# Two units per attention step on TensorE: outputs and scores of a pair taken together every eight places

## The chip, the cores and the metric

The kernel runs on one core of one Trainium2 chip. The metric is the device time of one launch in microseconds (us): 609.71 us before the change, the median of three runs (609.52 to 609.72). One further run was profiled; it took 609.88 us, and its profile spans 608.1 us from the first to the last instruction.

## The reference

Chunked attention with memory keys, then a dense two-layer block with a leaky rectifier (negative values are scaled by alpha). Everything is in float32.

```python
B, H, S, D = 4, 8, 768, 64          # chunk 32, 16 keys to the left, 8 to the right, 8 memory keys
for c in range(S // 32):
    q_c    = q[:, :, 32*c : 32*c+32]
    k_full = concat(mem_k, k[:, :, 32*c-16 : 32*c+40])     # cut at the ends of the sequence
    scores = q_c @ k_full.T / 8
    a      = exp(scores - max(scores)); a = a / (sum(a) + 1e-9)
    out[:, :, 32*c : 32*c+32] = a @ v_full
x = out.transpose(0, 2, 1, 3).reshape(3072, 512)
h = x @ w_in                                               # 512 -> 2048
g = max(h, 0) + alpha * min(h, 0)
y = g @ w_out                                              # 2048 -> 512
```

## The kernel before

The 3072 tokens are cut into 8 **blocks** of 384. A block's attention is cut into 4 **units** of two heads each, so there are 32 units; unit u belongs to block u // 4. The dense block works on one block of tokens and one 128-wide slice f of the 2048 hidden channels at a time; such a (block, f) is a **place**, and `ORDER` lists the 128 places. Blocks 0 and 1 are interleaved at first; from place 32 on each block has 16 places in a row. `PLACE` gives a place's number.

At a place TensorE makes an **up** (12 matmuls of 128x384, line 638, into one of two PSUM banks, h0 or h1 by the place's parity), ScalarE and VectorE make g from it (lines 647 and 650, then 656 and 660 split it into a high and a low part), and TensorE makes a **down** (9 matmuls of 128x512, line 668, into three banks o0 to o2). Full float32 precision comes from three products of high and low parts. From place `FIRST_RUN` on, places are asked for in runs of four: four ups follow each other, then the downs; four pairs of buffers for g's parts (`NSUM`) allow it.

Units 0 to 7 are done at the start by other functions (`windows`). Units 8 to 31 are each done in this way, in the midst of the places:

- **scores**: `head_products` (line 292) is 24 small float32 products (the trace shows each as two, 48 matmuls), one head into bank s0, the other into s1.
- **softmax**: `scores` (lines 301 to 331): VectorE hides the keys that lie outside (302 or 304), takes the maximum (313) for each head, negates it (316); ScalarE takes six exponentials (323), with their sums.
- **weights** and **turn** (lines 333 to 371): sums are inverted, GpSimd multiplies (343), and VectorE transposes the result in 14 pieces (364).
- **outputs**: `value_products` (line 378) is 8 products (16 matmuls in the trace) into bank `a`; `split` (lines 411 and 415) copies them into a high and a low part, the x that the ups of the unit's block read.

`attend` (line 385) is one **step** of TensorE: the outputs of an old unit, where there is one that is due, and then the scores of a new one. `BEGIN` and `LATER` say at which place a unit begins; its outputs are due `DUE_VALUES` = 4 places later. So from place 33 on there is a step every four places.

The order is fixed when the kernel is built. `Plan` (line 103) takes the steps with an engine, an estimated cost, keys read and written, and a `rest` (how much work is left from the place at which the step is due). `send` plays this through: on each engine it takes, of the steps that could run earliest, the one with the most work behind it. What comes out is a fixed order for each engine; each engine works in that order and waits on semaphores. A step that is due at a smaller place number goes ahead of others.

Of the kernel before, what the change touches and what calls it, by code (L numbers as in the profile page):

```python
# [9 lines left out]
F32 = mybir.dt.float32  # L10
F32R = mybir.dt.float32r
AF = mybir.ActivationFunctionType
ALU = mybir.AluOpType
AX = mybir.AxisListType
# [4 lines left out]
P = 128  # L19
B, H, S, D = 4, 8, 768, 64  # L20
NM = 8
CH, LEFT, RIGHT = 32, 16, 8
WIN = LEFT + CH + RIGHT
KW = WIN + NM
TQ = 96
NJ = TQ // CH
# [3 lines left out]
NT = BT // TQ  # L30
NPAIR = H // 2
# [4 lines left out]
NEG = -3.0e38  # L36
SCALE = 1.0 / 8.0
# [22 lines left out]
PE, DVE, ACT, POOL, SP = "PE", "DVE", "ACT", "POOL", "SP"  # L60
# [6 lines left out]
NJOINT, LAG = 9, 1  # L67
# [6 lines left out]
PLACE = {x: i for i, x in enumerate(ORDER)}  # L74
# [1 line left out]
PAIR = 4.7  # L76


BEGIN = {2: (4, 6, 8, 10)}

NSUM = 4
RUN, FIRST_RUN = 4, 32
LATER = (-3, 1, 5, 9)


STIR = (8, 2, 1)

DUE_WEIGHTS, DUE_VALUES = 3, 4


NWIN, NSET = 2 * NPAIR, 4
# [68 lines left out]
def body(ctx: ExitStack, tc: tile.TileContext, qvw, kw, first, w_in, w_out, alpha, out):  # L160
    nc = tc.nc
# [47 lines left out]
    def rest(place):  # L209
        return (len(ORDER) - place) * PAIR  # L210

    def begins(u):

        blk, i = divmod(u, NPAIR)
        if blk < 2:
            return blk
        return PLACE[(1, NJOINT - 1) if blk == 2 else (blk - 1, 0)] + BEGIN.get(blk, LATER)[i]

    def due(u, later=0):

        return rest(begins(u) + later)

    def sets(u):

# [2 lines left out]
    def e_keys(u):  # L227
        return [("e", u % 2, n) for n in range(NJ * 2)]

    def den_keys(u):  # L230
        return [("den", u % 3, n) for n in range(NJ * 2)]
# [15 lines left out]
    def load_v(u):  # L247
        blk, pr = divmod(u, NPAIR)

        def load():  # L250
            state[u]["v"] = ld.tile([P, NT, 2, D], F32, name="v_t")
            nc.sync.dma_start(out=state[u]["v"],
                              in_=qvw[blk, pr, :, BT:].rearrange("p (t h d) -> p t h d", t=NT, h=2))

        step(SP, 0.75, load, writes=["v"])

    def stir(t, num):

# [3 lines left out]
    def score_products(u):  # L262
# [8 lines left out]
        for n in range(2 * NJ):  # L271
            for i in range(2):
# [5 lines left out]
                    start=True, stop=True,  # L278
                )

    def head_products(u):

        st = state[u]
        st["s"] = [ps_s.tile([P, 512], F32, name="s_ps", tag=f"s{h2}")[:, :NJ * KW].rearrange("p (n k) -> p n k", n=NJ)
                   for h2 in range(2)]
        for n in range(NJ):
            for g in range(4):
                t, j = SLOT[(g, n)]
                c = t * NJ + j
                for h2 in range(2):  # L290
                    rows = slice(h2 * D, (h2 + 1) * D)
                    nc.tensor.matmul(  # L292
                        out=st["s"][h2][g * CH:(g + 1) * CH, n],
                        lhsT=qs[sets(u)][rows, c * CH:(c + 1) * CH],
                        rhs=kbs[sets(u)][rows, t, STARTS[j]:STARTS[j] + KW],
                        start=True, stop=True,
                    )

    def hide(u, s):

        if u // NPAIR % 2 == 0:
            nc.vector.memset(s[0:CH, 0, ..., 0:LEFT], NEG)
        else:
            nc.vector.memset(s[3 * CH:4 * CH, NJ - 1, ..., KW - RIGHT:KW], NEG)

    def scores(u):
        st = state[u]

        def top(h2):
            if h2 == 0:  # L310
                st["mx"] = sm.tile([P, NJ, 2], F32, name="mx", tag=f"mx{u % 3}")
            hide(u, st["s"][h2])
            nc.vector.tensor_reduce(out=st["mx"][:, :, h2], in_=st["s"][h2], axis=AX.X, op=ALU.max)

        def negate():
            nc.vector.tensor_scalar(out=st["mx"], in0=st["mx"], scalar1=-SCALE, scalar2=None, op0=ALU.mult)  # L316

        def exps(i):
            if i == 0:
                st["e"] = at.tile([P, NJ * 2, KW], F32, name="e", tag=f"e{u % 2}")  # L320
                st["den"] = sm.tile([P, NJ * 2, 1], F32, name="den", tag=f"den{u % 3}")
            n, h2 = divmod(i, 2)
            nc.scalar.activation(out=st["e"][:, i], in_=st["s"][h2][:, n], func=AF.Exp, scale=SCALE,  # L323
                                 bias=st["mx"][:, n, h2:h2 + 1], accum_out=st["den"][:, i])

        for h2 in range(2):
            step(DVE, 0.46, partial(top, h2), writes=[("s", h2), ("mx", u % 3)], rest=due(u))
        step(DVE, 0.16, negate, writes=[("mx", u % 3)], rest=due(u))
        for i in range(NJ * 2):
            step(ACT, 0.54, partial(exps, i), reads=[("s", i % 2), ("mx", u % 3)],  # L330
                 writes=[("e", u % 2, i), ("den", u % 3, i)] if i else e_keys(u) + den_keys(u), rest=due(u))

    def weights(u):
        st = state[u]

        def guard():
            nc.vector.tensor_scalar(out=st["den"], in0=st["den"], scalar1=1e-9, scalar2=None, op0=ALU.add)

        def inverse():
            nc.vector.reciprocal(out=st["den"], in_=st["den"])  # L340

        def scale():
            nc.gpsimd.tensor_tensor(out=st["e"], in0=st["e"], in1=st["den"].broadcast_to([P, NJ * 2, KW]),  # L343
                                    op=ALU.mult)

        def spread():
            nc.scalar.copy(out=zeroed["e2"][:, :, NM:NM + CH], in_=st["e"][:, :, :CH])

        step(DVE, 0.16, guard, writes=den_keys(u), rest=due(u, DUE_WEIGHTS))
        step(DVE, 0.19, inverse, writes=den_keys(u), rest=due(u, DUE_WEIGHTS))  # L350
        step(POOL, 0.86, scale, reads=den_keys(u), writes=e_keys(u), rest=due(u, DUE_WEIGHTS))
        step(ACT, 0.37, spread, reads=e_keys(u), writes=["e2"], rest=due(u, DUE_WEIGHTS))

    TURNS = [(g, j, n0, n1, t0) + piece
             for g in range(4)
# [4 lines left out]
    def turn(u):  # L360
        st = state[u]

        def go(g, j, n0, n1, t0, src, half, quad):
            nc.vector.transpose(  # L364
                out=pts[u % NPT][quad * CH:(quad + 1) * CH, j, t0:t0 + n1 - n0].rearrange("p t h q -> p (t h) q"),
                in_=(st["e"], zeroed["e2"])[src][g * CH:(g + 1) * CH, 2 * n0:2 * n1, half * CH:(half + 1) * CH],
            )

        for i, x in enumerate(TURNS):
            step(DVE, 0.37 if x[3] - x[2] > 1 else 0.235, partial(go, *x), reads=["e2"] if x[5] else e_keys(u),  # L370
                 writes=[("pt", u % NPT, i)], rest=due(u, DUE_WEIGHTS))

    def value_products(u):
        st = state[u]
        st["a"] = ps_a.tile([P, 512], F32, name="a_ps", tag="a")
        for t in range(NT):
            for h2 in range(2):
                nc.tensor.matmul(  # L378
                    out=st["a"][h2 * D:(h2 + 1) * D, t * TQ:(t + 1) * TQ],
                    lhsT=st["v"][:, t, h2, :],  # L380
                    rhs=pts[u % NPT][:, :, t, h2, :],
                    start=True, stop=True,
                )

    def attend(place, olds, news):

        def products():
            for u in olds:
                value_products(u)
            for u in news:  # L390
                head_products(u)

        reads, writes = [], []
        for u in olds:
            reads += ["v"] + [("pt", u % NPT, i) for i in range(len(TURNS))]
            writes.append("a")
        for u in news:
            reads += [("q", sets(u)), ("k", sets(u))]
            writes += [("s", 0), ("s", 1)]
        step(PE, 0.85 * len(olds) + 0.67 * len(news) - (0.2 if olds and news else 0.0), products, reads=reads, writes=writes,  # L400
             rest=rest(place))

    def split(u, ak="a"):

# [325 lines left out]
    def unit_begins(u):  # L730
        if u < NWIN:
            windows(u)
        else:
            scores(u)
        if u < NWIN and u + NSET < NWIN:
            load_first(u + NSET)
        elif u >= NWIN - NKB and u + NKB < NU:
            load_unit(u + NKB)
# [11 lines left out]
    step(POOL, 3.0, zero, writes=["e2"] + [("pt", i, j) for i in range(NPT) for j in range(len(TURNS))] + [("ew", i) for i in range(NPT)])  # L750
    for f in range(NF - NSET, NF):
        load_w(f)
    load_v(NWIN)

    todo = {}
    for u in range(NWIN, NU):
        todo.setdefault(begins(u), []).append((u, 0))
        todo.setdefault(begins(u) + DUE_WEIGHTS, []).append((u, 1))
        todo.setdefault(begins(u) + DUE_VALUES, []).append((u, 2))
    down = done = None  # L760
    o_ps = {}
    for blk, f in ORDER:
# [13 lines left out]
        if olds or news:  # L776
            attend(PLACE[blk, f], olds, news)
        for u in olds:
            split(u)
            if u + 1 < NU:  # L780
                load_v(u + 1)
        for u in news:
            unit_begins(u)
        for u, part in now:
            if part == 1:
                weights(u)
                turn(u)
        o = o_ps.setdefault((blk, f1), [])
        down = partial(add_down, o)
        if f == f1 - 1:  # L790
# [57 lines left out]
```

## Time and profile before

| | |
|---|---|
| median of three runs | 609.71 us |
| the profiled execution | 609.88 us, span 608.1 us |
| TensorE matmul (PE) | 600.4 us busy, 99% of the span |
| VectorE (DVE) | 399.0 us, 66% |
| ScalarE (ACT) | 212.2 us, 35% |
| GpSimd (POOL) | 33.9 us, 6% |
| granted TensorE clock | 1.0 |

In the profile a row of a group names the line, the engine, the operation, output<-input and the count, then after the bar the busy time, the mean duration and the idle time before the group's instructions. PEld is TensorE's weight load. A matmul's duration in the trace is longer than the time until the next may start, since matmuls overlap; so what a piece of work costs TensorE is read from the start of one piece to the start of the next, as the chain of work that ended last lists it.

### The profile page before, as it was taken

The numbers are of one execution on the slowest core, as the hardware profiler recorded it, in microseconds if no ns is written. First come the engines' busy times: TensorE is split into PE (matmuls) and PEld (weight loads), VectorE is DVE, ScalarE is ACT, GpSimd is POOL, SyncE is SP. The second block draws the span as 40 slices with busy tenths as digits, with TensorE's granted clock in tenths as the row PEclk, the third lists the DMA queues.
The fourth block names the chain that finished last, engine by engine and source line by source line (L and its number), as shares of the span: only waits on it lengthen the run. The fifth ranks groups of instructions, "written<-read, shape, count | busy, mean of one in ns | idle before, by whom it ended". The sixth has DMA issues, their size and how long they took to land.

```text
span 608.1 us, 11545 instructions
## 1 busy us (share of the span) xinstructions
PE 600.4 (99%) x4618; PEld 532.0 (87%) x4622; DVE 399.0 (66%) x1012; ACT 212.2 (35%) x596; POOL 33.9 (6%) x61
## 2 busy tenths in 40 slices
PE   8999999999999999999999999999999999999997
PEld 5789989888888898998889998898998898999986
DVE  5888999868887667476665756577555767434331
ACT  3688887545222222421223221222222222121111
POOL 3410000001000000000000000000000000000000
PEclk9999999999999999999999999999999999999999
DMA  8999400014131011311012111111112000010001
GB/s 335 355 408 408 176 0 1 23 43 150 51 119 49 3 48 50 101 50 50 3 49 101 50 50 50 53 50 50 50 50 87 18 16 19 1 52 1 0 1 52
DMA packets 20934, 48.99 MB, mean 81 GB/s; under 512 B 2448, under 2 KB 5520, under 8 KB 20880
## 3 DMA queue, kind: packets, MB, share of 16 engines
q1 hardware_dynamic: 20880, 48.25, 22.4%
q8 instruction: 36, 0.59, 0.4%
q14 instruction: 18, 0.15, 0.1%
HBM read 41.95 MB, written 6.29 MB: 79 GB/s over the span
## 4 chain that ended last, share of the span: by engine, by line
PE 94%; DMA 3%; DVE 2%; ACT 0%; issue 0%; SPq 0%; ACTq 0%
PE h_ps L638 44%; PE o_ps L668 43%; PE a_ps L378 3%; PE s_ps L292 3%; DMA w_t<-w_in 2%; DMA early<-first 1%; DVE w_t L571 0%; DVE xl L415 0%; SPq L427 0%; DVE den L458 0%; DVE a L575 0%; DVE w_t L567 0%; DVE mx L446 0%; DVE e L450 0%; PE s_ps L274 0%
## 5 line engine op out<-in xcount | busy, mean ns | idle before, releaser
L638 PE MATMUL h_ps<-xh,w 128*128 128x384 f32 x1024 | 260.9, 335 | 0.3 <-DVE w L586 0.3
L668 PE MATMUL o_ps<-w,gh 128*128 128x512 f32 x768 | 238.2, 391 | 0.0
L638 PEld LDWEIGHTS h_ps<-xh,w 128*128 128x128 f32 x1024 | 185.4, 188 | 2.6 <-DVE w L586 0.6
L638 PE MATMUL h_ps<-xl,w 128*128 128x384 f32 x512 | 174.6, 341 | 0.1
L668 PEld LDWEIGHTS o_ps<-w,gh 128*128 128x128 f32 x768 | 144.1, 188 | 29.1
L647 ACT ACTIVATE g<-h_ps 128x384 f32<-128x384 f32 x128 | 64.1, 501 | 289.8 <-PE h_ps L638 289.6
L650 DVE SCALAR_TENSOR_TENSOR g<-g,rise,h_ps 128x384 f32<-128x384 f32 x128 | 78.4, 613 | 130.0 <-ACT g L647 129.0
L668 PE MATMUL o_ps<-w,gl 128*128 128x512 f32 x384 | 149.8, 390 | 0.0
L364 DVE STREAM_TRANSPOSE pt<-e 32x192 f32<-32x192 f32 (+1 forms) x336 | 99.5, 301 | 6.7 <-POOL e L343 1.8
L638 PEld LDWEIGHTS h_ps<-xl,w 128*128 128x128 f32 x512 | 96.1, 188 | 4.5 <-DVE xl L415 0.3
L668 PEld LDWEIGHTS o_ps<-w,gl 128*128 128x128 f32 x384 | 72.1, 188 | 14.1
L660 DVE TENSOR_TENSOR gl<-g,gh 128x384 fp32r<-128x384 f32 x128 | 70.1, 548 | 3.8 <-ACT gh L656 1.5
L323 ACT ACTIVATE e<-s_ps,mx 128x64 f32<-128x64 f32 x144 | 43.0, 324 | 6.6 <-DVE mx L316 6.6
L343 POOL TENSOR_TENSOR e<-e,den 128x384 f32<-128x384 f32 x24 | 19.9, 830 | 455.6 <-DVE den L340 435.3
L656 DVE CAST gh<-g 128x384 fp32r<-128x384 f32 x104 | 37.3, 360 | 7.7 <-PE o_ps L668 3.3
L323 ACT ACTIVATION_READ_ACCUMULATOR e<-s_ps,mx 128x1 f32 x144 | 31.3, 218 | 0.0
L715 ACT COPY o_t<-o_ps 128x512 f32<-128x512 f32 x21 | 12.2, 588 | 48.5 <-PE o_ps L668 47.3
L378 PEld LDWEIGHTS a_ps<-pt,v_t 128*64 128x64 f32 x384 | 16.6, 136 | 6.1 <-issue 6.1
L411 ACT CAST xh<-a_ps 128x384 fp32r<-128x384 f32 x32 | 15.4, 481 | 16.8 <-PE a_ps L378 14.8
L378 PE MATMUL a_ps<-pt,v_t 128*64 128x96 f32 x384 | 21.1, 252 | 0.0
L559 ACT ACTIVATE a<-w_t 128x1024 f32<-128x1024 f32 (+1 forms) x18 | 18.8, 1050 | 4.1 <-DMA w_t<-w_in 3.0
L575 DVE SCALAR_TENSOR_TENSOR a<-a,w_t 128x1024 int32<-128x1024 int32 (+1 forms) x18 | 19.8, 1102 | 0.2
(52 smaller groups left out, 283.6 us busy)
## 6 DMA issues: line engine op xcount, KB each, us to landing
w_t<-w_in SPq DMA_DIRECT2D x16, 512.0 KB, 10.2
w_t<-w_out SPq DMA_DIRECT2D x16, 512.0 KB, 10.2
qk<-kw SPq DMA_DIRECT2D x24, 272.0 KB, 3.8
v_t<-qvw SPq DMA_DIRECT2D x24, 256.0 KB, 2.7
out<-o_t SPq DMA_DIRECT2D x24, 256.0 KB, 2.1
early<-first SPq DMA_DIRECT2D x8, 656.0 KB, 6.2
qk<-qvw SPq DMA_DIRECT2D x24, 192.0 KB, 3.9
early<-first SPq DMA_DIRECT2D x8, 256.0 KB, 6.9
```

Source lines behind the costliest of these rows:

```text
L323: nc.scalar.activation(out=st["e"][:, i], in_=st["s"][h2][:, n], func=AF.Exp, scale=SCALE, bias=st["mx"][:, n, h2:h2 + 1], accum_out=st["d ...
L343: nc.gpsimd.tensor_tensor(out=st["e"], in0=st["e"], in1=st["den"].broadcast_to([P, NJ * 2, KW]), op=ALU.mult)
L364: nc.vector.transpose(out=pts[u % NPT][quad * CH:(quad + 1) * CH, j, t0:t0 + n1 - n0].rearrange("p t h q -> p (t h) q"), in_=(st["e"], zer ...
L378: nc.tensor.matmul(out=st["a"][h2 * D:(h2 + 1) * D, t * TQ:(t + 1) * TQ], lhsT=st["v"][:, t, h2, :], rhs=pts[u % NPT][:, :, t, h2, :], sta ...
L559: nc.scalar.activation(out=d["a"].bitcast(F32), in_=t[:, :, :, 1].bitcast(F32), func=AF.Copy, scale=REBIAS)
L575: nc.vector.scalar_tensor_tensor(out=d["a"], in0=d["a"], scalar=3, in1=d["t"][:, :, :, 1], op0=ALU.logical_shift_left, op1=ALU.bitwise_or)
L638: nc.tensor.matmul(out=h["ps"][:, :BT], lhsT=ws[f, 0][:, wk, k * P:(k + 1) * P], rhs=xs[first + k][xk], start=(k == 0 and n == 0), stop=(k ...
L647: nc.scalar.activation(out=h["g"], in_=h["ps"][:, :BT], func=AF.Relu, scale=-1.0)
L650: nc.vector.scalar_tensor_tensor(out=h["g"], in0=h["g"], scalar=rise[:, f:f + 1], in1=h["ps"][:, :BT], op0=ALU.mult, op1=ALU.add)
L656: copy(out=h["gh"], in_=h["g"])
L660: nc.vector.tensor_tensor(out=h["gl"], in0=h["g"], in1=h["gh"].bitcast(F32), op=ALU.subtract)
L668: nc.tensor.matmul(out=o_ps[tt], lhsT=h[gk][:, tt * P:(tt + 1) * P], rhs=ws[f, 1][:, wk], start=(f == first_f and i == 0), stop=(f == last ...
```

## The change

From unit 12 on (block 3), two units are taken together. `attend` is called with up to two old and two new units: outputs, outputs, scores, scores. The scores of both units lie side by side in the banks s0 and s1 (`banks`), so that one memset and one maximum per head serve both, and one negation. The second unit's outputs go to bank h1, one of the two banks of the ups; they leave it by the same `split`. Pairs begin at the places 0 and 6 of block 2 and, later, 4 places before and 4 after a block's start, so there is a step every eight places. It is asked for 0.2 places ahead of its place, where it was asked for at its place. V has two buffers in place of one. `FIRST_RUN` goes from 32 to 24, and the estimated costs of the steps and the due times are set anew.

```diff
-BEGIN = {2: (4, 6, 8, 10)}
+BEGIN = {2: (4, 6, 8, 10), 3: (0, 6)}
...
-RUN, FIRST_RUN = 4, 32
-LATER = (-3, 1, 5, 9)
+RUN, FIRST_RUN = 4, 24
+FIRST_FRONT = 12
+LATER = (-4, 4)
...
-DUE_WEIGHTS, DUE_VALUES = 3, 4
+DUE_WEIGHTS, DUE_VALUES = {1: 3, 2: 4}, {1: 4, 2: 8}
...
+    def size(u):
+        return 1 if u < 3 * NPAIR else 2
...
-        return rest(begins(u) + later)
+        return rest(begins(u) + later + (1.8 if u >= FIRST_FRONT else 0))
...
-            state[u]["v"] = ld.tile([P, NT, 2, D], F32, name="v_t")
+            state[u]["v"] = ld.tile([P, NT, 2, D], F32, name="v_t", tag=f"v{u % 2}")
...
+    def banks(us):
+        n = len(us)
+        ss = [ps_s.tile([P, 512], F32, name="s_ps", tag=f"s{h2}")[:, :n * NJ * KW].rearrange("p (u n k) -> p u n k", u=n, n=NJ)
+              for h2 in range(2)]
+        for i, u in enumerate(us):
+            state[u]["s"] = [s[:, i] for s in ss]
+        state[us[0]]["all"] = ss
...
-    def scores(u):
+    def scores(us):
...
-            hide(u, st["s"][h2])
-            nc.vector.tensor_reduce(out=st["mx"][:, :, h2], in_=st["s"][h2], axis=AX.X, op=ALU.max)
+            s = state[us[0]]["all"][h2]
+            hide(us[0], s)
+            nc.vector.tensor_reduce(out=d["mx"][:, :, :, h2], in_=s, axis=AX.X, op=ALU.max)
...
-            step(DVE, 0.46, partial(top, h2), writes=[("s", h2), ("mx", u % 3)], rest=due(u))
-        step(DVE, 0.16, negate, writes=[("mx", u % 3)], rest=due(u))
-        for i in range(NJ * 2):
-            step(ACT, 0.54, partial(exps, i), reads=[("s", i % 2), ("mx", u % 3)],
-                 writes=[("e", u % 2, i), ("den", u % 3, i)] if i else e_keys(u) + den_keys(u), rest=due(u))
+            step(DVE, 0.26 + 0.21 * len(us), partial(top, h2), writes=[("s", h2), mk], rest=due(us[0]))
+        step(DVE, 0.17, negate, writes=[mk], rest=due(us[0]))
+        for u in us:
+            for i in range(NJ * 2):
+                step(ACT, 0.54, partial(exps, u, i), reads=[("s", i % 2), mk],
+                     writes=[("e", u % 2, i), ("den", u % 3, i)] if i else e_keys(u) + den_keys(u), rest=due(u))
...
     def value_products(u):
         st = state[u]
-        st["a"] = ps_a.tile([P, 512], F32, name="a_ps", tag="a")
+        pool, tag = (ps_h, "h1") if u % size(u) else (ps_a, "a")
+        st["a"] = pool.tile([P, 512], F32, name="a_ps", tag=tag)
...
             for u in olds:
                 value_products(u)
+            if news:
+                banks(news)
             for u in news:
                 head_products(u)
...
-        step(PE, 0.85 * len(olds) + 0.67 * len(news) - (0.2 if olds and news else 0.0), products, reads=reads, writes=writes,
-             rest=rest(place))
+        step(PE, 0.31 + 0.53 * len(olds) + 0.48 * len(news), products, reads=reads, writes=writes,
+             rest=rest(place - (0.2 if (olds + news)[-1] >= FIRST_FRONT else 0)))
...
-        todo.setdefault(begins(u) + DUE_WEIGHTS, []).append((u, 1))
-        todo.setdefault(begins(u) + DUE_VALUES, []).append((u, 2))
+        todo.setdefault(begins(u) + 1, []).append((u, 1))
+        todo.setdefault((begins(u) + DUE_VALUES[size(u)] if size(u) == 1 or u + 2 >= NU else begins(u + 2)), []).append((u, 2))
...
         for u in olds:
-            split(u)
-            if u + 1 < NU:
-                load_v(u + 1)
-        for u in news:
-            unit_begins(u)
+            split(u, "h1" if u % size(u) else "a")
+            if u + 2 < NU:
+                load_v(u + 2)
         for u, part in now:
             if part == 1:
                 weights(u)
                 turn(u)
+        for u in news:
+            unit_begins(u)
```

How the built order moves, in two places. First TensorE, at one step in the later blocks. `a_ps` is the outputs, `s_ps` the scores, `h_ps` an up, `o_ps` a down. Before, with a step behind the first up of a run:

```order
L638 MATMUL h_ps<-xh,w 128x384 x2
L638 MATMUL h_ps<-xl,w 128x384
L638 MATMUL h_ps<-xh,w 128x384 x2
L378 MATMUL a_ps<-pt_637,v_t 64x96 x8
L292 MATMUL s_ps<-qk_155 32x64 x24
L638 MATMUL h_ps<-xl,w 128x384
L638 MATMUL h_ps<-xh,w 128x384 x2
```

And TensorE of the changed kernel, at the first step with two old and two new units:

```order
L689 MATMUL o_ps<-w,gl 128x512
L689 MATMUL o_ps<-w,gh 128x512 x2
L397 MATMUL a_ps<-pt_637,v_t 64x96 x8
L397 MATMUL a_ps<-pt_639,v_t 64x96 x8
L306 MATMUL s_ps<-qk_154 32x64 x24
L306 MATMUL s_ps<-qk_155 32x64 x24
L689 MATMUL o_ps<-w,gl 128x512
```

Over the whole order there were 26 steps: 22 with outputs and scores, 2 with outputs alone and 2 with scores alone. There are now 17: 9 with two outputs and two scores, 1 with two scores alone, 1 with two outputs alone, and 6 that are still single (2 with both, 2 with outputs, 2 with scores). In the later blocks the step stands between the downs of one run and the first up of the next, where it stood behind the first up. No instruction of TensorE is added or left out.

Second VectorE, behind one such step (numbers tell buffers apart). Before, where `a_ps_3852` is the unit's outputs:

```order
L304 MEMSET s_ps_3861 32x8
L313 TENSOR_REDUCE mx_3909<-s_ps_3861 128x3
L660 TENSOR_TENSOR gl_3913<-g_3887,gh_3903 128x384
L304 MEMSET s_ps_3862 32x8
L313 TENSOR_REDUCE mx_3909<-s_ps_3862 128x3
L415 TENSOR_TENSOR xl_3918<-a_ps_3852,xh_3905 128x384
L316 TENSOR_SCALAR mx_3909<-mx_3909 128x6
L650 SCALAR_TENSOR_TENSOR g_3933<-g_3933,rise_151,h_ps_3890 128x384
```

And VectorE of the changed kernel, where `a_ps_3409` is the second unit's outputs, in bank h1, and `h_ps_3468` is the first up behind the step, in h0:

```order
L318 MEMSET s_ps_3418 32x2x8
L329 TENSOR_REDUCE mx_3484<-s_ps_3418 128x6
L436 TENSOR_TENSOR xl_3489<-a_ps_3409,xh_3481 128x384
L318 MEMSET s_ps_3419 32x2x8
L329 TENSOR_REDUCE mx_3484<-s_ps_3419 128x6
L436 TENSOR_TENSOR xl_3496<-a_ps_3400,xh_3487 128x384
L332 TENSOR_SCALAR mx_3484<-mx_3484 128x12
L671 SCALAR_TENSOR_TENSOR g_3511<-g_3511,rise_151,h_ps_3468 128x384
```

The outputs in bank h1 are taken out between the two maxima, ahead of those in bank `a`. The second up behind the step is the one that writes h1 next.

More of the change, by code (lines that the diff above doesn't have):

```diff
@@ L216, in begins @@
             return blk
-        return PLACE[(1, NJOINT - 1) if blk == 2 else (blk - 1, 0)] + BEGIN.get(blk, LATER)[i]
+        return PLACE[(1, NJOINT - 1) if blk == 2 else (blk - 1, 0)] + BEGIN.get(blk, LATER)[i // size(u)]
     def due(u, later=0):
-        return rest(begins(u) + later)
+        return rest(begins(u) + later + (1.8 if u >= FIRST_FRONT else 0))
     def sets(u):
@@ L250, in load @@
         def load():
-            state[u]["v"] = ld.tile([P, NT, 2, D], F32, name="v_t")
+            state[u]["v"] = ld.tile([P, NT, 2, D], F32, name="v_t", tag=f"v{u % 2}")
             nc.sync.dma_start(out=state[u]["v"],
                               in_=qvw[blk, pr, :, BT:].rearrange("p (t h d) -> p t h d", t=NT, h=2))
-        step(SP, 0.75, load, writes=["v"])
+        step(SP, 0.75, load, writes=[("v", u % 2)])
     def stir(t, num):
@@ L279, in score_products @@
                 )
+    def banks(us):
[5 more added lines that the diff above has]
+        state[us[0]]["all"] = ss
     def head_products(u):
         st = state[u]
-        st["s"] = [ps_s.tile([P, 512], F32, name="s_ps", tag=f"s{h2}")[:, :NJ * KW].rearrange("p (n k) -> p n k", n=NJ)
-                   for h2 in range(2)]
         for n in range(NJ):
@@ L301, in hide, with exps @@
         if u // NPAIR % 2 == 0:
-            nc.vector.memset(s[0:CH, 0, ..., 0:LEFT], NEG)
+            nc.vector.memset(s[0:CH, :, 0, 0:LEFT], NEG)
         else:
-            nc.vector.memset(s[3 * CH:4 * CH, NJ - 1, ..., KW - RIGHT:KW], NEG)
-    def scores(u):
-        st = state[u]
+            nc.vector.memset(s[3 * CH:4 * CH, :, NJ - 1, KW - RIGHT:KW], NEG)
+    def scores(us):
+        d = {}
+        mk = ("mx", us[0] // len(us) % 2)
         def top(h2):
             if h2 == 0:
-                st["mx"] = sm.tile([P, NJ, 2], F32, name="mx", tag=f"mx{u % 3}")
-            hide(u, st["s"][h2])
-            nc.vector.tensor_reduce(out=st["mx"][:, :, h2], in_=st["s"][h2], axis=AX.X, op=ALU.max)
+                d["mx"] = sm.tile([P, len(us), NJ, 2], F32, name="mx", tag=f"mx{len(us)}{mk[1]}")
+            s = state[us[0]]["all"][h2]
+            hide(us[0], s)
+            nc.vector.tensor_reduce(out=d["mx"][:, :, :, h2], in_=s, axis=AX.X, op=ALU.max)
         def negate():
-            nc.vector.tensor_scalar(out=st["mx"], in0=st["mx"], scalar1=-SCALE, scalar2=None, op0=ALU.mult)
-        def exps(i):
+            nc.vector.tensor_scalar(out=d["mx"], in0=d["mx"], scalar1=-SCALE, scalar2=None, op0=ALU.mult)
+        def exps(u, i):
+            st = state[u]
             if i == 0:
@@ L323, in exps @@
             nc.scalar.activation(out=st["e"][:, i], in_=st["s"][h2][:, n], func=AF.Exp, scale=SCALE,
-                                 bias=st["mx"][:, n, h2:h2 + 1], accum_out=st["den"][:, i])
+                                 bias=d["mx"][:, u - us[0], n, h2:h2 + 1], accum_out=st["den"][:, i])
         for h2 in range(2):
-            step(DVE, 0.46, partial(top, h2), writes=[("s", h2), ("mx", u % 3)], rest=due(u))
-        step(DVE, 0.16, negate, writes=[("mx", u % 3)], rest=due(u))
-        for i in range(NJ * 2):
-            step(ACT, 0.54, partial(exps, i), reads=[("s", i % 2), ("mx", u % 3)],
-                 writes=[("e", u % 2, i), ("den", u % 3, i)] if i else e_keys(u) + den_keys(u), rest=due(u))
+            step(DVE, 0.26 + 0.21 * len(us), partial(top, h2), writes=[("s", h2), mk], rest=due(us[0]))
[4 more added lines that the diff above has]
+                     writes=[("e", u % 2, i), ("den", u % 3, i)] if i else e_keys(u) + den_keys(u), rest=due(u))
     def weights(u):
@@ L347, in spread @@
             nc.scalar.copy(out=zeroed["e2"][:, :, NM:NM + CH], in_=st["e"][:, :, :CH])
[L349 to L352, printed above, removed]
+        step(DVE, 0.16, guard, writes=den_keys(u), rest=due(u, DUE_WEIGHTS[size(u)]))
+        step(DVE, 0.19, inverse, writes=den_keys(u), rest=due(u, DUE_WEIGHTS[size(u)]))
+        step(POOL, 0.86, scale, reads=den_keys(u), writes=e_keys(u), rest=due(u, DUE_WEIGHTS[size(u)]))
+        step(ACT, 0.37, spread, reads=e_keys(u), writes=["e2"], rest=due(u, DUE_WEIGHTS[size(u)]))
     TURNS = [(g, j, n0, n1, t0) + piece
@@ L370, in turn @@
             step(DVE, 0.37 if x[3] - x[2] > 1 else 0.235, partial(go, *x), reads=["e2"] if x[5] else e_keys(u),
-                 writes=[("pt", u % NPT, i)], rest=due(u, DUE_WEIGHTS))
+                 writes=[("pt", u % NPT, i)], rest=due(u, DUE_WEIGHTS[size(u)]))
     def value_products(u):
         st = state[u]
-        st["a"] = ps_a.tile([P, 512], F32, name="a_ps", tag="a")
+        pool, tag = (ps_h, "h1") if u % size(u) else (ps_a, "a")
+        st["a"] = pool.tile([P, 512], F32, name="a_ps", tag=tag)
         for t in range(NT):
@@ L394, in attend @@
         for u in olds:
-            reads += ["v"] + [("pt", u % NPT, i) for i in range(len(TURNS))]
-            writes.append("a")
+            reads += [("v", u % 2)] + [("pt", u % NPT, i) for i in range(len(TURNS))]
+            writes.append("h1" if u % size(u) else "a")
         for u in news:
@@ L733, in unit_begins @@
         else:
-            scores(u)
+            if u % size(u) == 0:
+                scores(list(range(u, u + size(u))))
         if u < NWIN and u + NSET < NWIN:
@@ L752, in body @@
         load_w(f)
-    load_v(NWIN)
+    for u in range(NWIN, NWIN + 2):
+        load_v(u)
     todo = {}
```

## The prediction

> **What bounds the kernel now.** I read the page's busy times first, then its slices, then the chain that ended last.
>
> ```profile
> PE 600.4 (99%) x4618; PEld 532.0 (87%) x4622; DVE 399.0 (66%) x1012; ACT 212.2 (35%) x596; POOL 33.9 (6%) x61
> ...
> DVE  5888999868887667476665756577555767434331
> PEclk9999999999999999999999999999999999999999
> ...
> PE 94%; DMA 3%; DVE 2%; ACT 0%; issue 0%; SPq 0%; ACTq 0%
> ```
>
> TensorE is busy all the time, at the full granted clock, and is 94% of the chain. VectorE is nearly full in the first quarter (slices of 15.2 us) and at five to seven tenths later. Whether TensorE ever waits is asked of the groups of its instructions between 60 and 604 us (idle time is the last number):
>
> ```profile
> L638 PE MATMUL h_ps<-xh,w 128*128 128x384 f32 x962 | 245.0, 335 | 0.0
> L668 PE MATMUL o_ps<-w,gh 128*128 128x512 f32 x737 | 228.6, 391 | 0.0
> L378 PE MATMUL a_ps<-pt,v_t 128*64 128x96 f32 x384 | 21.1, 252 | 0.0
> L292 PE MATMUL s_ps<-qk 64*32 64x64 f32 x1152 | 17.4, 223 | 0.0
> ```
>
> No group waits. So from 60 us on the time is the sum of what TensorE issues, and a change there is worth what it does to that sum, as long as no new wait comes. Busy time overlaps, so the price of a step is read from the chain, whose pieces follow each other:
>
> ```profile
> 116.65 2.11 PE h_ps L638 x12
> 118.76 0.66 PE s_ps L292 x45
> 119.42 2.26 PE o_ps L668 x9
> 121.68 2.10 PE h_ps L638 x12
> 123.78 2.08 PE o_ps L668 x9
> ...
> 291.65 8.20 PE o_ps L668 x36
> 299.85 2.11 PE h_ps L638 x12
> 301.96 0.81 PE a_ps L378 x16
> 302.77 0.65 PE s_ps L292 x45
> 303.43 6.45 PE h_ps L638 x36
> ...
> 518.53 4.19 PE h_ps L638 x24
> 522.72 0.81 PE a_ps L378 x16
> 523.53 4.37 PE h_ps L638 x24
> ...
> 538.14 8.34 PE h_ps L638 x48
> ```
>
> (It lists 45 of the 48 small matmuls; three are put in the piece before.) Four ups alone take 8.34 us. With a step of outputs and scores among them they take 2.11+0.81+0.65+6.45 = 10.02, so such a **step costs 1.68 us**. With outputs alone 4.19+0.81+4.37 = 9.37: **1.03**. Scores alone, against an up and a down without a step: (2.11+0.66+2.26) − (2.10+2.08) = **0.85**. These prices hold the way in and out: the array leaves its large matmuls and returns to them.
>
> **What a second unit adds.** The 16 matmuls of the outputs and the 48 of the scores, counted up to a time in the step at 301.89 us:
>
> ```profile
> 301.88:302.04 0.16, 0.15 (x4) 1.00 0.00 0
> 301.88:302.53 0.65, 0.64 (x16) 1.00 0.00 0
> ...
> 302.70:302.94 0.24, 0.24 (x32) 1.00 0.00 0
> 302.70:303.21 0.51, 0.51 (x48) 1.00 0.00 0
> ```
>
> Outputs: behind the first four, 12 begin in 0.49 us, 41 ns each. A unit that follows another of its kind needs no way in, so its 16 cost 16 × 0.041 = **0.66 us**, which I take; the upper bound is the whole piece of the chain, 0.81.
>
> Scores: 32 begin in 0.24 us (7.5 ns each), the other 16 in 0.27 (16.8 ns each, with a pause in it). A second unit's 48 would all follow behind the fast 32. The lower bound is 48 × 0.0075 = 0.36 us, the upper 48 × 0.0168 = 0.81. The weight loads of these matmuls tell which is nearer:
>
> ```profile
> 302.69:303.04 0.35, 0.34 (x35) 1.00 0.00 0
> 302.69:303.13 0.44, 0.43 (x46) 1.00 0.00 0
> ```
>
> Behind the pause 11 begin in 0.09 us, 8.2 ns each, and each has one matmul. So the pause is paid once, and 48 more cost 48 × 0.0083 = **0.40 us**; this is what I take. The page "TensorE: Matmul & The Clock Gate" of the Trainium skill (its table of specifications) gives TensorE a queue of 64 instructions. By that rule the fast 32, with 32 weight loads, are what had been queued, and a second unit runs at the rate of the refill, the same 0.40; the trace's count of 32 agrees.
>
> **The change part by part.** The built order has 26 steps before: 22 with both, 2 with outputs alone, 2 with scores alone. Before: 22×1.68 + 2×1.03 + 2×0.85 = 40.7 us. After, A being the second outputs' price and S the second scores': 2 single steps with both (3.36), 2 with outputs (2.06), 2 with scores (1.70), one with two scores (0.85+S), one with two outputs (1.03+A), nine with two of each (15.12+9A+9S); together 24.1 + 10(A+S). The gain is 16.6 − 10(A+S). With A = 0.66 and S = 0.40 it is **6.0 us**; with S = 0.36, 6.4; with A = 0.66 and S = 0.81, 1.9; with both at 0.81, 0.4.
>
> *The place of the step* moves from behind an up to behind a down; the way in is paid either way, and the boundary between a down and an up, which the step now covers, is worth little: four ups and four downs take 8.34+8.20 = 16.54 in a run, and four places one by one 4 × (2.10+2.08) = 16.72, so 0.18 us for six more changes between the two, 0.03 each. *FIRST_RUN* at 24 asks for eight more places in runs, but the old order had grouped many of them by itself: over the whole program the ups and downs come in 98 stretches where they came in 102. That is 4 × 0.03 = 0.1 us, which I leave out.
>
> *VectorE* loses work: a memset and a maximum of 192 elements for each unit and head, against one of 384 for two units.
>
> ```profile
> L446 DVE TENSOR_REDUCE mx<-s_ps 128x6 f32<-128x384 f32 x8 | 4.5, 558 | 0.3
> ...
> L313 DVE TENSOR_REDUCE mx<-s_ps 128x3 f32<-128x192 f32 x48 | 17.2, 359 | 1.6
> ```
>
> 2 × 0.36 becomes 0.56 (line 446 has that size), so ten pairs save about 20 × 0.16 = 3 us on an engine that bounds nothing here: nothing. *ScalarE and GpSimd* do the same work in larger lumps. Twelve exponentials come after a step; at their price, with their sums,
>
> ```profile
> L323 ACT ACTIVATE e<-s_ps,mx 128x64 f32<-128x64 f32 x144 | 43.0, 324 | 6.6 <-DVE mx L316 6.6
> L323 ACT ACTIVATION_READ_ACCUMULATOR e<-s_ps,mx 128x1 f32 x144 | 31.3, 218 | 0.0
> ```
>
> that is at most 12 × 0.54 = 6.5 us in a stretch of eight places (two runs, 33.1 us, and the step). In the built order the rectifiers of the ups stand between them. *The loads* are doubled up on SP's queue, but a pair's q, k and v are asked for as the pair before leaves TensorE, eight places ahead; nothing.
>
> **The new wait** is at bank h1. The second up behind a step writes it and must wait for line 436 (415 before) to have read the second outputs. In the old step the same read went like this on VectorE:
>
> ```profile
> 303.68 0.07 DVE L304 MEMSET s_ps<- 32x8 f32 x1
> 303.77 0.36 DVE L313 TENSOR_REDUCE mx<-s_ps 128x3 f32<-128x192 f32 x1
> 304.05 0.55 DVE L660 TENSOR_TENSOR gl<-g,gh 128x384 fp32r<-128x384 f32 x1
> 304.98 0.55 DVE L415 TENSOR_TENSOR xl<-a_ps,xh 128x384 fp32r<-128x384 f32 x1
> ```
>
> In the new order it stands third: memset 0.07, maximum 0.56, difference 0.55, so about 1.3 us after the scores are there. The first up goes on meanwhile, 2.1 us. There is some 0.8 us in hand, and no other work of VectorE stands ahead that isn't long done (the last up of the run before lies at least three downs back). I cost it at nothing; if that cover is gone, every microsecond late is 1 us for each of ten places.
>
> *Sum.* 609.88 − 6.0 = 603.9 for an execution like the profiled one, which lies 0.17 above the median; so **603.7 us** for the median.
>
> **The rivals.**
>
> *Second scores at the slow mean.* If the pause comes again and again, S = 0.81 and A = 0.66: gain 1.9, 607.8 us. For it: the mean behind the fast 32 is 16.8 ns. Against: the loads' 8.2 ns behind the pause.
>
> *Nothing saved by the pairing.* If a second unit pays a whole piece for the outputs (0.81) and the slow mean for the scores, the gain is 0.4: 609.3, no change. For it only that the bank changes between the units, and in the old trace no unit follows another.
>
> *Uneven loads on VectorE and ScalarE.* Pairs bring 28 transposes at once. In the built order 23 of them stand in one row behind a run's last g:
>
> ```profile
> L364 DVE STREAM_TRANSPOSE pt<-e 32x192 f32<-32x192 f32 x168 | 61.8, 368 | 4.2 <-POOL e L343 1.8
> L364 DVE STREAM_TRANSPOSE pt<-e 32x64 f32<-32x64 f32 x168 | 37.6, 233 | 2.4
> ```
>
> 9 × 0.368 + 14 × 0.233 = 6.6 us. What they must not delay is the next run's first rectification: four downs (8.20) and an up (2.1) later, less about 2 us for the last g, 8.3 us; 1.7 in hand. If they are late by 2 us each time, TensorE waits some 0.3 us in each of ten periods: 606.7.
>
> *Bank h1 late: slower.* If VectorE reads h1 last (behind the second maximum, the other difference, the negation and the first up's rectification, 0.07+0.56+0.55+0.16+0.61 = 1.95 us later), the second up waits 1.95 − 0.8 = 1.15 us, ten times: 603.7 + 11.5 = 615.2. It turns the sign once the wait is over 0.6 us a step. For it: that bank is one of the two that the ups turn over, and the scheduler's prices for a step are below the trace's. Against: the order of the rows, and that a step longer than planned gives VectorE more time.
>
> *A floor for small matmuls: slower.* The start of one matmul could be bound by a fixed time in a long stream. The same page (section "Back-to-back issue gap") states a floor of about 25 ns however small the matmul. By that, as an estimate, S = 48 × 0.025 = 1.2 us and A+S = 1.86: 609.7 + 2.0 = 611.7. This case's 32 in 0.24 us disagree with it, so it gets little.
>
> **How the numbers follow.** Forecast 0.72; slow mean 0.10; uneven loads 0.06; nothing saved 0.05; bank h1 0.04; the floor 0.03. A measurement of this kernel can tell about 0.2%, 1.2 us, from no change. The forecast, the slow mean and the uneven loads are faster: 0.88. Nothing saved: 0.05. The last two are slower: 0.07. The forecast's own bounds are 603.3 (S = 0.36) to 605.2 (A at 0.81); the range goes to 602.9, for the boundaries that I put at nothing, and up to 607.8, the slow mean: it leaves out what lies above, 0.12, and a little below.
>
> **What would show it right or wrong.** In the changed profile's chain, a step with two of each should be 0.66 longer in its outputs and 0.40 in its scores: outputs 1.47, scores 1.05, nine times, and the four ups behind it 8.5 (8.34, and the 0.19 that 6.45 has over three quarters of 8.34). In the count of one step's scores, 32 in 0.24 us, one pause, and then 8 ns each up to 96; a second pause would be the slow mean. TensorE's groups should have no idle time from 60 us on; a wait of line 659 for VectorE's line 436 is bank h1, a wait of line 659 for line 671 is the uneven load. VectorE's busy time should fall by some 3 us. The forecast is wrong if the nine steps are each more than 2.9 us, or if TensorE waits at all behind them.

## The result, and the profile after

The changed kernel takes **605.29 us**, the median of six runs (605.08 to 605.43); the kernel before took 609.72 (six runs, 609.52 to 610.38). The ratio is 0.9926, with a 95% interval of 0.9916 to 0.9936: 4.4 us faster. The forecast was 603.7 us, 6.0 faster, with a range from 602.9 to 607.8.

The page of the changed kernel, whose lines answer to those shown of before:

```profile
span 603.7 us, 11483 instructions
...
PE 596.3 (99%) x4622; PEld 531.0 (88%) x4622; DVE 397.7 (66%) x962; ACT 214.1 (35%) x596; POOL 35.7 (6%) x61
```

TensorE's groups between 60 and 600 us, with the idle time last:

```profile
L659 PE MATMUL h_ps<-xh,w 128*128 128x384 f32 x962 | 244.7, 335 | 0.0
...
L397 PE MATMUL a_ps<-pt,v_t 128*64 128x96 f32 x384 | 18.9, 250 | 0.0
L306 PE MATMUL s_ps<-qk 64*32 64x64 f32 x1152 | 15.5, 224 | 0.0
```

In none of these groups does TensorE wait: it is still the sum of what it issues. The chain that ended last, through one run of places (start, us, piece):

```profile
261.56 1.47 PE a_ps L397 x32
263.03 1.17 PE s_ps L306 x81
264.20 8.52 PE h_ps L659 x48
```

The two units' outputs are 1.47 us, as worked out (0.81 + 0.66). The scores are 1.17, where 1.05 was expected (0.65 + 0.40). The ups behind them take 8.52, as expected. The same scores, counted up to a time in the step:

```profile
262.96:263.20 0.24, 0.24 (x32) 1.00 0.00 0
262.96:263.48 0.52, 0.51 (x48) 1.00 0.11 32
262.96:263.60 0.64, 0.64 (x62) 1.00 0.09 26
262.96:264.00 1.03, 1.03 (x96) 1.00 0.05 16
```

The first unit is what it was: 32 in 0.24 us, 48 in 0.51. The second unit's 48 take 0.52 us more, not 0.40. Seven of the ten steps are like this one, 1.02 to 1.03 us from the first start of the 96 to the last; the other three take 1.06 to 1.16. In the longest, at 226.90, no matmul of the scores begins between 0.52 and 0.65 us.

```profile
226.90:227.42 0.52, 0.52 (x48) 1.00 0.00 0
226.90:227.55 0.65, 0.65 (x48) 1.00 0.00 0
226.90:228.06 1.16, 1.16 (x95) 1.00 0.00 0
```

There the stop is between the two units, and the two others above 1.03 us have a shorter one (0.06 and 0.07 us) at the same point. In the step at 262.96, as in the six others like it, there is no such gap: 48 have begun after 0.51 us and 62 after 0.64. What all ten have is one instruction of TensorE's queue that only waits (PEldq). In the step at 262.96 it is the only one from 0.25 to 0.94 us into the scores:

```profile
L306 PEldq EVENT_SEMAPHORE  x1: 51/51/51, 263.4 to 263.4; - x1
```

It stands at 0.42 us in the steps like this one and at 0.46, 0.47 and 0.55 us in the three longer ones, and in all ten the second unit's first matmul begins 0.11 us behind it. Why it comes later in three of them is open. In the built program it belongs to the second unit's q and k, which come by two transfers of their own. What it waits for was done long before: the transfers for the step at 262.96 were asked for behind the step ahead of it,

```profile
227.66 2.08 SPq L249 DMA_DIRECT2D qk<-kw  x2
...
230.73 0.91 SPq L246 DMA_DIRECT2D qk<-qvw  x2
```

and the last of them had landed at 235.5, 27 us before the step.

### The profile page after: what moved, and what is told of

Its sections match the earlier page's. It is cut to its first block, busy times and chain, and to the rows that moved or that the text cites. A ratio compares the mean times of both kernels' runs of the same rounds, so it can differ in the third digit from the quotient of the medians.

```text
span 603.7 us, 11483 instructions
## 1 busy us (share of the span) xinstructions
PE 596.3 (99%) x4622; PEld 531.0 (88%) x4622; DVE 397.7 (66%) x962; ACT 214.1 (35%) x596; POOL 35.7 (6%) x61
## 4 chain that ended last, share of the span: by engine, by line
PE 96%; DMA 2%; DVE 1%; ACT 0%; issue 0%; SPq 0%; ACTq 0%
PE h_ps L659 44%; PE o_ps L689 44%; PE a_ps L397 3%; PE s_ps L306 2%; DMA early<-first 1%; DMA w_t<-w_in 1%; PE s_ps L267 1%; PE s_ps L281 1%; PE a_ps L517 1%; DVE w_t L588 0%; PE o_ps L504 0%; DVE w_t L592 0%; DVE xl L436 0%; DVE a L596 0%; ACT a L580 0%
## 5 line engine op out<-in xcount | busy, mean ns | idle before, releaser
L681 DVE TENSOR_TENSOR gl<-g,gh 128x384 fp32r<-128x384 f32 x128 | 72.2, 565 | 4.8 <-ACT gh L677 1.9
L361 POOL TENSOR_TENSOR e<-e,den 128x384 f32<-128x384 f32 x24 | 22.2, 924 | 436.7 <-DVE den L358 436.7
L365 ACT COPY e<-e 128x192 f32<-128x192 f32 x24 | 8.4, 352 | 47.0 <-DVE pt L382 41.4
L436 DVE TENSOR_TENSOR xl<-a_ps,xh 128x384 fp32r<-128x384 f32 x32 | 17.5, 549 | 10.0 <-ACT xh L432 10.0
```

The source lines that it names most:

```text
L436: nc.vector.tensor_tensor(out=xl, in0=st["a"][:, :BT], in1=st["xh"].bitcast(F32), op=ALU.subtract)
L681: nc.vector.tensor_tensor(out=h["gl"], in0=h["g"], in1=h["gh"].bitcast(F32), op=ALU.subtract)
```

## Experiments

Beside the versions with joint loads and with bank h0 the kernel before took 609.44 us, beside the others 609.71; so 0.3 us between versions of the two groups mean little.

Two theories of the 0.12 us and more that a second unit's scores pay beyond their price. **W**: the wait instruction between the units, though what it waits for is done. **Q**: a long stream of small matmuls, or the change to another unit's operands, pauses by itself.

### The waits ahead of both units

```diff
-    def head_products(u):
+    def head_products(u, places):
...
-        for n in range(NJ):
-            for g in range(4):
+        for n, g in places:
+            for _ in range(1):
...
-            for u in news:
-                head_products(u)
+            grid = [(n, g) for n in range(NJ) for g in range(4)]
+            ahead = 1 if len(news) > 1 else 0
+            if ahead:
+                head_products(news[1], grid[:1])
+            for i, u in enumerate(news):
+                head_products(u, grid[1:] if i else grid)
```

> The changed kernel with one edit: in a step with two new units the second unit's first product for each head is issued ahead of the first unit's 24, so that TensorE meets the waits for the second unit's loads of q and k at the start of the scores, not between the two units. Theory W (the 0.52 to 0.65 us that the second scores cost, against 0.40 worked out, hold a wait instruction between the units): the 96 matmuls begin within 0.91 us in place of 1.02 to 1.16, ten times about 0.14, so 1.4 us less: 603.9 us. Theory Q (a long stream of small matmuls pauses by itself whenever the queue has run dry): nothing changes, 605.3 us, and the 96 still take 1.02 us and more.

Measured: 605.12 us (605.02 to 605.7, five runs; ratio 0.9926, 0.9914 to 0.9939). No gain, so by its words the result speaks for Q. The count within a step:

```profile
262.41:262.71 0.30, 0.30 (x31) 1.00 0.00 0
262.41:263.48 1.07, 1.07 (x96) 1.00 0.06 15
```

The 96 take 1.06 us in nearly every step: the irregular long ones are gone, but the first 32 now take 0.30 us in place of 0.24. In the trace no instruction that only waits stands among the 96 of any step any more. So the edit did what it was meant to, and the order in which it puts the products costs about as much as it took away. What in that order costs it stays open. The edit adds a change from the second unit's operands to the first's behind the first few matmuls, but the widest gaps between starts stand behind the 24th, 31st and 35th.

### The same operands for both units

The second unit's scores are made from the first unit's q and k; what is computed is then not the reference's, with the work unchanged.

```diff
-                        lhsT=qs[sets(u)][rows, c * CH:(c + 1) * CH],
-                        rhs=kbs[sets(u)][rows, t, STARTS[j]:STARTS[j] + KW],
+                        lhsT=qs[sets(u - u % size(u))][rows, c * CH:(c + 1) * CH],
+                        rhs=kbs[sets(u - u % size(u))][rows, t, STARTS[j]:STARTS[j] + KW],
```

> The changed kernel with the second unit's scores made from the first unit's q and k (so the second unit of each pair gets the wrong scores; the amount of work is the same). The second unit then has no load of its own to wait for, and no wait stands anywhere in the scores but at their start. Theory W: as with the waits ahead, the 96 matmuls begin within 0.91 us and the time is 603.9 us. Theory Q: 1.02 us and more, 605.3 us.

Measured: 603.79 us (603.65 to 603.87, four runs; ratio 0.9902, 0.9889 to 0.9916).

```profile
262.19:262.43 0.24, 0.24 (x32) 1.00 0.00 0
262.19:263.15 0.96, 0.96 (x96) 1.00 0.07 17
```

All ten steps take 0.96 us. A long stream in this order does not pause by itself for another 0.1 us, then. But wait and change of operands went together here, so the two were still to be parted.

### One transfer for both units

q of both units comes by one transfer and k of both by another, into one tile. The second unit reads its own operands, with nothing of its own to wait for. The result is the reference's.

```diff
-    qk = [const.tile([P, BT + NT * NKT], F32, name=f"qk{i}") for i in range(NKB)]
+    qk2 = const.tile([P, NKB, BT + NT * NKT], F32, name="qk2")
+    qk = [qk2[:, i] for i in range(NKB)]
...
+    def load_pair(u):
...
+        def load_q():
+            nc.sync.dma_start(out=qk2[:, :, :BT], in_=qvw[blk, pr:pr + 2, :, :BT].rearrange("u p x -> p u x"))
+        def load_k():
+            nc.sync.dma_start(out=qk2[:, :, BT:], in_=kw[blk, pr:pr + 2].rearrange("u p t k -> p u (t k)"))
...
+            elif u % 2:
+                load_pair(u + NKB - 1)
```

> The changed kernel with q of both units of a pair loaded by one transfer and k of both by another, into one tile. The result is the same, the order of TensorE is the same, and the second unit reads its own q and k, but there is nothing of its own to wait for between the units. Theory W (the wait instruction between the units is what the second scores pay beyond the rate): the 96 matmuls begin within 0.96 us, as with the same operands, against 1.02 to 1.16 before; ten times 0.09, so 604.4 us or a little less. Theory O (what costs is that the operands change to another tile; the kernel with the same operands removed that along with the wait): 1.02 us and 605.2 us.

Measured: **603.86 us** (603.69 to 604.32, four runs; ratio 0.9907, 0.9892 to 0.9922). The count in a step, and the chain:

```profile
262.21:262.45 0.24, 0.24 (x32) 1.00 0.30 68
262.21:262.69 0.48, 0.48 (x49) 1.00 0.15 34
262.21:263.17 0.96, 0.96 (x96) 1.00 0.08 17
```

```profile
260.81 1.47 PE a_ps L411 x32
262.28 1.10 PE s_ps L320 x72
```

The instructions that only wait, at the scores' line, in the changed kernel and here:

```profile
L306 PEldq EVENT_SEMAPHORE  x38: 51/51/51, 112.8 to 479.0; - x38
```

```profile
L320 PEldq EVENT_SEMAPHORE  x28: 51/51/51, 112.5 to 476.3; - x28
```

Ten fewer, one for each double step. 49 matmuls have begun after 0.48 us, where it had been 48 after 0.51, and all ten steps take 0.95 to 0.96 us. So theory W holds in this order of the products: the operands change between the units here too, and without the wait the 96 are 0.07 to 0.20 us shorter. Summed over the ten steps that is 0.9 us (9.5 us against 10.5 in the trace's starts). The median fell by 1.4, or by some 1.2 when each kernel is set against the kernel before beside it. In the profiled executions, 1.8 us apart, TensorE's part from 60 us to its end is 1.1 shorter, of which the scores are 0.9; 0.3 lie ahead of 60 us, where both kernels do the same, and 0.4 at the close (below).

### The kinds apart

The order within a double step: outputs, scores, outputs, scores.

```diff
-            for u in olds:
-                value_products(u)
             if news:
                 banks(news)
-            for u in news:
-                head_products(u)
+            for i in range(max(len(olds), len(news))):
+                if i < len(olds):
+                    value_products(olds[i])
+                if i < len(news):
+                    head_products(news[i])
```

> The changed kernel with the work of a double step in another order: outputs, scores, outputs, scores, in place of outputs twice and then scores twice. It has as many steps and as many instructions. If the gain comes from units of one kind following each other (each change of kind costs a way in), a double step costs two pieces of 0.81 + 0.65 and one 0.22 for leaving and returning, 3.14 us against about 2.87 measured in the changed kernel, nine times: 605.3 + 2.4 = 607.7 us. If it comes from the smaller number of steps, from leaving the large matmuls less often, it is 605.3 us or less (the second unit's wait for its loads falls into its outputs, which may give back some 0.14 us a step: 604.0).

Measured: 607.95 us (607.51 to 608.07, six runs; ratio 0.9967, 0.9956 to 0.9978), as the prices have it. The chain:

```profile
261.97 0.81 PE a_ps L397 x16
262.78 0.66 PE s_ps L306 x45
263.44 0.81 PE a_ps L397 x16
264.25 0.65 PE s_ps L306 x45
```

The step costs whole pieces again, 0.81 and 0.65 twice, though the large matmuls are left as seldom as in the changed kernel. Of its 4.4 us some 2.7 hang on units of one kind following each other, and 1.8 on there being fewer steps. By TensorE's part alone, from 60 us to its end in the profiled executions, the shares are nearer to each other: 2.5 and 2.3, because the close takes some of the second back (below).

### Runs from place 32 on

```diff
-RUN, FIRST_RUN = 4, 24
+RUN, FIRST_RUN = 4, 32
```

> The changed kernel with one part undone: runs of four places are asked for from place 32 on, as before the change, not from 24. The prediction gave this part less than 0.1 us. Expected 605.2 to 605.5 us. If the earlier runs were worth their upper bound (0.05 us a place for eight places), 605.7 us; if they had brought a wait in the quarter in which VectorE is full, less than 605.2.

Measured: 605.16 us (605.11 to 605.64, five runs; ratio 0.9926, 0.9913 to 0.994). This part of the change is worth nothing that can be measured.

### The second outputs in bank h0

```diff
-        pool, tag = (ps_h, "h1") if u % size(u) else (ps_a, "a")
+        pool, tag = (ps_h, "h0") if u % size(u) else (ps_a, "a")
...
-            writes.append("h1" if u % size(u) else "a")
+            writes.append("h0" if u % size(u) else "a")
...
-            split(u, "h1" if u % size(u) else "a")
+            split(u, "h0" if u % size(u) else "a")
```

> The changed kernel with the second outputs in bank h0 in place of h1. The first up behind a step at a run's start would write h0 and wait for its read, some 1.3 us; the scheduler sees that and puts the step behind an up of h0 and a down instead, so that the next up is one of h1. By the prices that costs two more changes between ups and downs for a pair, 10 x 2 x 0.03 = 0.6 us: 605.9 us. If the read of the bank is later than the scheduler thinks (VectorE reads it between the two maxima), TensorE waits for it and the time is 607 us or more.

Measured: 605.77 us (605.73 to 606.0, four runs; ratio 0.9938, 0.9922 to 0.9955), as expected. The scheduler put an up and a down ahead of the step, so that the bank was not the next to be written:

```profile
258.82 2.10 PE h_ps L659 x12
260.93 2.09 PE o_ps L689 x9
263.01 1.47 PE a_ps L397 x32
264.49 1.17 PE s_ps L306 x82
265.65 6.47 PE h_ps L659 x36
```

The step itself costs the same 1.47 and 1.17 (its last piece, 6.47, is three ups; with the up ahead that makes four). The time is 0.5 us above the changed kernel's, about what ten further changes from an up to a down and back were priced at (0.6). That the wait at h0 would have cost more was not tried.

### Joint loads, and block 2 in pairs

If a pair of units costs less than two single steps, then so do units 8 to 11, which the change left single. On top of the joint loads, block 2 begins in pairs too.

```diff
-BEGIN = {2: (4, 6, 8, 10), 3: (0, 6)}
+BEGIN = {2: (4, 9), 3: (0, 6)}
...
-        return 1 if u < 3 * NPAIR else 2
+        return 1 if u < 2 * NPAIR else 2
```

The outputs of units 10 and 11 are made due 5 places after their scores.

> Joint loads as above, and the units 8 to 11 (block 2) taken in pairs too, beginning at places 21 and 26. By the measured prices three steps fewer: 2x0.85 + 2x1.68 + 2x1.03 = 7.1 us becomes (0.85+0.45) + (1.68+0.66+0.45) + (1.03+0.66) = 5.8, so 1.3 us less than with joint loads alone: 603.1 us, if TensorE waits for nothing. Rival: in that stretch VectorE is full, and the read of bank h1 and the rectifications come late; TensorE then waits for lines of VectorE by about as much as is saved: 604.4 us or more.

Measured: **602.13 us** (601.99 to 602.28, four runs; ratio 0.9877, 0.9863 to 0.9892). This is the fastest version, 7.3 us under the 609.44 that the kernel before took beside it. Its chain shows the new double steps of block 2, at the prices of the joint loads, and its groups between 60 and 596 us show that no wait came with them:

```profile
116.15 1.10 PE s_ps L320 x72
...
142.41 1.47 PE a_ps L411 x32
143.89 1.10 PE s_ps L320 x72
...
166.03 1.10 PE s_ps L320 x72
167.13 1.47 PE a_ps L411 x32
```

```profile
L673 PE MATMUL h_ps<-xh,w 128*128 128x384 f32 x960 | 244.2, 335 | 0.0
```

It gained 1.7 us over the joint loads alone, where 1.3 was expected. In the profiled executions 1.4 of it lie in TensorE's part from 60 us on, 0.2 ahead of that and 0.1 at the close. The sum had missed a saving of 0.2: it priced the scores at 166.03 and the outputs at 167.13 as two steps (0.85 and 1.03 for the first unit of each), but they stand side by side, which is one step of 1.68. With it 1.5 was to be expected from TensorE, and 1.4 came.

## Why the prediction was right, and where it was not

*What bounds the kernel.* Right. TensorE's part shortened by about what the time fell by (4.8 and 4.4, below), and no group of TensorE waits after 60 us in the changed kernel or in the versions whose groups are shown.

*Second outputs, A = 0.66.* Right: 0.81 + 0.66 = 1.47, and 1.47 is in the chain.

*Second scores, S = 0.40.* **This is the term that was mis-sized.** It measured 0.54 on average over the ten steps: the 96 starts take from 1.02 to 1.16 us, where the first unit's 48 take 0.51. Ten times 0.14 is 1.4 us, and 6.0 − 1.4 = 4.6, against 4.4 measured; that they are so near is in part luck (see the time around the sum). The part of it that is a cause shown by runs: with no wait between the units (joint loads) the 96 take 0.955, 0.09 a step less. So the step that failed is "*The loads* … nothing". The transfers were indeed early, but the argument asked only whether the data would be late. The wait for them stands in TensorE's queue whether they are late or not, and in this stream it costs something even when they are long done. What is left without the wait is 0.955 − 0.51 = 0.45, which is 0.05 a step more than the 0.40. The last 48 of the 96 take 0.48 us there, 10 ns each and not the 8.3 that 11 weight loads behind one pause had given, and the first 48 are 0.03 shorter than a unit's scores alone. Why, no run looked into.

*One pause, then 8 ns each.* The one pause is right without the wait, but the matmuls behind it take 10 ns each. No run tested whether the fast 32 are what had been queued, as the prediction reads them. The slow mean as a rival (S = 0.81) is out in every step: the longest gives 1.16 − 0.51 = 0.65.

*A pause paid once.* That the second unit must follow the first of its kind for the low price is shown by the kinds apart, where every piece cost its whole price again (0.81, 0.66, 0.81, 0.65) and 2.7 us of the gain went (2.5 by TensorE's part alone).

*FIRST_RUN and the boundaries.* Put at nothing; taking FIRST_RUN back to 32 changed the median by 0.1.

*Bank h1.* Right, with the hand as worked out. VectorE and TensorE of the changed kernel, behind the step at 262.96:

```profile
264.26 0.09 DVE L316 MEMSET s_ps<- 32x32 f32 x1 [6.62 <-PE s_ps L306]
264.38 0.56 DVE L329 TENSOR_REDUCE mx<-s_ps 128x6 f32<-128x384 f32 x1
264.86 0.55 DVE L436 TENSOR_TENSOR xl<-a_ps,xh 128x384 fp32r<-128x384 f32 x1
```

```profile
266.33 0.33 PE L659 MATMUL h_ps<-xl,w 128*128 128x384 f32 x1
```

Bank h1 is read in the third place and free at 265.41; the second up begins at 266.33. So 0.9 us are in hand, where 0.8 was expected, and the slower rival (615.2) didn't come about.

*Uneven loads on VectorE and ScalarE.* They cost nothing, as forecast: no idle time in TensorE's groups.

*VectorE saves some 3 us.* Wrong in size, without a consequence: 399.0 to 397.7, 1.3 less. The memsets, maxima and negations did become fewer (1012 instructions to 962), but another group grew, before and after:

```profile
L660 DVE TENSOR_TENSOR gl<-g,gh 128x384 fp32r<-128x384 f32 x128 | 70.1, 548 | 3.8 <-ACT gh L656 1.5
```

```profile
L681 DVE TENSOR_TENSOR gl<-g,gh 128x384 fp32r<-128x384 f32 x128 | 72.2, 565 | 4.8 <-ACT gh L677 1.9
```

The same 128 subtractions took 17 ns more each, 2.1 us in all. About half of that is nine subtractions of 670 to 691 ns, and these nine begin while GpSimd's multiplication (line 361) runs; before the change none ran beside one. The other half was not examined.

*Time around the sum.* The prediction set everything outside TensorE's sum equal in both kernels. In the profiled executions the end isn't. One down at 60 us and the last piece of the chain, the copy of the last result, in the kernel before, the changed kernel and the one with joint loads:

```profile
60.21 2.08 PE o_ps L668 x9
...
604.48 0.59 ACT o_t L715
```

```profile
60.18 2.08 PE o_ps L689 x9
...
599.62 0.59 ACT o_t L736
```

```profile
59.88 2.08 PE o_ps L703 x9
...
598.25 0.59 ACT o_t L750
```

Between the two lie 544.3, 539.4 and 538.4 us. So TensorE's part became 4.8 us shorter by the change, 0.2 more than 6.0 − 1.4. That remainder is of the size of what the prediction put at nothing for the boundaries, and was not taken apart. From the last copy to the end of the span (608.1, 603.7 and 601.9) are 3.6, 4.1 and 3.7 us, so the close took almost 0.5 back. Two small errors that point opposite ways make 4.6 and 4.4 look nearer than the account is. Of the joint loads' gain over the changed kernel, 0.4 lies in the close and not in the scores. What makes the close longer or shorter stays open.

*The other rivals.* "Nothing saved by the pairing" (609.3) fell with A and S. The floor for small matmuls (611.7) fell with the 32 scores that still begin in 0.24 us and the 96 in 0.96 without the wait, 10 ns each. The Trainium skill (page "TensorE: Matmul & The Clock Gate", section "Back-to-back issue gap") states that floor as about 25 ns; these counts disagree with it.

## What to carry to other kernels

In a kernel that is the sum of what one engine issues, small work costs its way in: put pieces of one kind behind each other, and price the second from the rate behind the way in, not from the whole piece. Then look for what stands in the stream besides the work: a wait for something long done is not free in the middle of many tiny matmuls, and one transfer for both pieces takes it away. Measure the whole count of the joined piece, since the price worked out from 11 weight loads was a tenth too low even without the wait.

## What the runs showed of the hardware that was not expected

- **A wait that is already satisfied costs TensorE time in a stream of small matmuls.** With the second unit's wait between the units, the 96 scores took 1.02 to 1.16 us; without it, 0.95 to 0.96 in all ten steps. In all ten steps the second unit's first matmul begins 0.11 us behind the waiting instruction, however late that stands. The first unit's scores have waits of that kind ahead of them too (0.9 us ahead in the step at 262.96), and their first 32 begin in 0.24 us in the changed kernel and in the one with joint loads alike. Moving the second wait ahead as well gained nothing in the one order that was tried (1.06 us).
- **The close of a launch differed between the profiled executions**, 3.6 to 4.1 us from the last copy to the end of the span, though the stores are the same. Each kernel was profiled once, so whether it goes by kernel or by execution isn't known; 0.4 us is a third of what the joint loads won.
- **GpSimd's multiplication became slower** without a change in it: 830 ns each before, 924 in the changed kernel (below). The trace shows when: 18 of the 24 take 879 ns or more, and each of these 18 overlaps a subtraction of VectorE (line 681); of the six at 830 ns only one does. Before, all 24 take 828 to 832 ns and none overlaps such a subtraction. With bank h0 ten are slow, and again each of them overlaps one. TensorE doesn't wait for the multiplication, so the time doesn't show it. No run was made to keep the two apart.

```profile
L343 POOL TENSOR_TENSOR e<-e,den 128x384 f32<-128x384 f32 x24 | 19.9, 830 | 455.6 <-DVE den L340 435.3 <-DVE mx L316 12.9 <-ACT xh L411 7.4
```

```profile
L361 POOL TENSOR_TENSOR e<-e,den 128x384 f32<-128x384 f32 x24 | 22.2, 924 | 436.7 <-DVE den L358 436.7
```
